# Reordering a head's softmax pipeline and its tail, with the output weights loaded in long rows, in a decode attention and MLP kernel

## The chip, the cores and the metric

The kernel runs on one core of one Trainium2 chip. The metric is the device time of one execution in microseconds (us). Executions of one kernel agree within about 0.4%.

## The reference, cut to what matters

```
x: 4 x 576;  32 query heads, 16 key/value heads, head size 128, last 2048 of 8192 positions
xn = layernorm(x)
q  = xn @ wq                                  # 576 x 4096
o  = softmax(q k^T / sqrt(128)) v             # per batch and head
A  = o.reshape(4, 4096) @ wo                  # 4096 x 576
B  = xn + gelu(layernorm(xn) @ w3) @ w4       # with one token the shifted branch is zero
out = x + A + B
```

Inputs and output are bf16. Little is computed with each byte. K and V alone are 67.1 MB, the weights about 20 MB.

## The kernel before: the parts that matter

K and V come in tiles of 2 MB, one per key/value head. Each of 128 partitions receives 16384 contiguous bytes. A head goes through three stages in three successive rounds of one loop. In round `t` K of head `t` is transposed on DVE and multiplied with q into a score bank. The softmax of head `t-1` runs, with its exponentials on ACT, and V of head `t-2` is multiplied on PE. The names in the profile: `kn` and `vn` are the tiles of K and V, `kt` is K transposed, `S` a score bank in PSUM (the memory that PE writes to), `mx`, `mxT` and `m` are steps of the maximum, `dg` is a diagonal of minus the maximum, which a matmul subtracts from `S`, `pt` are the exponentials, `O` the V products, `on` the normalised head output and `acc` the sum of the output. The mask matmul opens a score bank and writes a large negative number where query and key belong to different batches. DVE is VectorE, ACT is ScalarE, PE is TensorE and PEld its weight load.

```python
kvp = ctx.enter_context(tc.tile_pool(name="kv", bufs=NKV))                 # 7
ps_s = ctx.enter_context(tc.tile_pool(name="ps_s", bufs=2, space=PSUM))    # score banks
wo_src = A_wo.rearrange("(h d) n -> d h n", d=P)
def load_wo(p):              # 8 heads; a partition gets 8 separate rows of 1152 B
    t = wop.tile([P, WOH, D], BF16, tag="wo", name="wo_sb")
    nc.sync.dma_start(out=t[:], in_=wo_src[:, p * WOH:(p + 1) * WOH, :])
# ... cut ...
def pv(h, s):                # a quarter of the V products needs all four groups of exponentials
    for c in range(s * SC, (s + 1) * SC):
        nc.tensor.matmul(out=O_ps[h][:, 0:NJ], lhsT=vn[:, c, :], rhs=pt[:, c, :], ...)
# ... cut ...
for t in range(Hkv + LAG + 1):
    hm = t - 1; hv = t - LAG                    # LAG = 2
    for s in range(NSL):                        # four quarters
        if t < Hkv:
            k_transpose(t, s)                   # DVE, 3 kt buffers
            if s == 0: k_mask(t)                # PE, first write of head t's score bank
            k_scores(t, s)                      # PE
        if 0 <= hv - 1 < Hkv and s == 0: o_norm(hv - 1)
        if 0 <= hm < Hkv:
            if s == 0: sm_max(hm)               # DVE
            elif s == 1: sm_maxT(hm)            # PE mxT, DVE m and dg
            elif s == 2: sm_sub(hm); sm_exp(hm, 0); sm_exp(hm, 1)
            else: sm_exp(hm, 2); sm_exp(hm, 3)  # 16 exponentials in all, ACT
        if 0 <= hv < Hkv: pv(hv, s)
        if 0 <= hv - 1 < Hkv and s == 0: o_proj(hv - 1)
        # ... the MLP's first half runs in round 7 ...
for lo, hi in zip(W4_PIECES, W4_PIECES[1:]):
    mlp_out(lo, hi)                             # w4, in 5 pieces, after all heads
```

In the timelines below each engine runs its instructions in the order of these calls (PE runs L255, L275, L285 as the loop has them), so where a call stands in this loop decides what it may hold up.

## Time and profile before

| | before |
|---|---|
| time, median of 3 | 225.9 us |
| span of the profiled execution | 224.6 us |
| bytes read | 87.17 MB |
| last data packet of w4 lands (packet records of the trace) | 213.7 us |
| last w4 matmul ends | 221.4 us |
| mask matmul to mask matmul, heads 9 to 15 | 10.27 us |

The first lines are from the page: busy time of each engine with its share of the span.

```profile
span 224.6 us, 6358 instructions
...
PE 121.2 (54%) x2861; PEld 93.1 (41%) x2861; DVE 114.6 (51%) x214; ACT 70.3 (31%) x258; POOL 4.1 (2%) x13
```

No compute engine is busy for more than 54%. The view by windows gives, for each stretch of time, busy time by engine, the granted clock, the share of the 16 DMA engines' time and the rate. Here are stretches with a wo load (25 to 35 and 166 to 176 us), one with caches only, and the end.

```profile
core 0: us, PE busy (x) PEld busy (x) DVE busy (x) ACT busy (x) POOL busy (x), PEclk, DMA share, GB/s
25.00:35.00 10.00, 5.41 (x105) 3.58 (x105) 8.74 (x15) 1.28 (x1) 0.00 (x0) 1.00 1.03 399
36.00:56.00 20.00, 10.60 (x250) 7.75 (x250) 11.87 (x18) 8.59 (x32) 0.00 (x0) 1.00 1.00 424
166.00:176.00 10.00, 5.77 (x148) 4.45 (x147) 6.24 (x10) 4.30 (x16) 0.00 (x0) 1.00 1.04 404
208.00:214.00 6.00, 2.94 (x64) 2.07 (x61) 1.02 (x5) 4.30 (x16) 0.00 (x0) 1.00 0.53 219
214.00:224.60 10.60, 6.66 (x225) 5.97 (x222) 0.90 (x4) 0.00 (x0) 0.00 (x0) 0.98 0.01 4
```

The loads are saturated until 208 us, at 424 GB/s, or about 400 where wo's small packets are among them. Then come more than 10 us in which nearly nothing is loaded. The Trainium skill (page "Perfetto Trace Analysis", Engine Utilization, Roofline) puts the ceiling of a lone core at about 435 GB/s by its DMA engines. This trace, at 424 to 427, is near it.

Two rounds of the timeline show how a head's work hangs together. The columns are start and duration in us, engine, line and operation, and in brackets the idle time before it and who ended it.

```profile
171.25 4.47 ACT L292 ACTIVATE pt<-S 32x128 bf16<-32x128 f32 x16 [5.81 <-issue]
...
173.39 0.68 DVE L270 TENSOR_REDUCE mx<-S 128x8 f32<-128x512 f32 x1
...
175.77 0.58 PE L255 MATMUL S<-negbig,ohT 4*128 4x512 bf16 x1 [2.99 <-ACT pt L292]
...
178.14 0.37 PE L275 MATMUL mxT<-ident_f,mx 128*8 128x128 f32 x1
...
178.55 0.28 DVE L277 TENSOR_REDUCE m<-mxT 8x1 f32<-8x128 f32 x1 [3.33 <-PE mxT L275]
...
179.00 3.48 DVE L249 STREAM_TRANSPOSE kt<-kn 128x1024 int32<-128x1024 int32 x3
...
180.83 0.60 PE L285 MATMUL S<-dg,ones_bf 8*128 8x512 bf16 x1
...
181.51 4.47 ACT L292 ACTIVATE pt<-S 32x128 bf16<-32x128 f32 x16 [5.80 <-issue]
...
186.04 0.58 PE L255 MATMUL S<-negbig,ohT 4*128 4x512 bf16 x1 [3.00 <-ACT pt L292]
```

This is a ring. The exponentials end, and the mask matmul (L255), which waited 3.0 us for its bank, starts. Scores and mxT (L275) follow on PE, then m on DVE, which waited 3.3 us for it. Then come transposes, the subtraction (L285) and the next exponentials, 10.27 us later. Two cache tiles take 2 x 2.097 MB / 425 GB/s = 9.87 us, so this ring is slower than the loads. The chain of waits that ended last agrees: exponentials, the last V products, and all of w4 in one lump.

```profile
213.42 0.28 ACT pt L292
...
215.88 0.41 PE O L303 x16
...
217.17 4.28 PE acc L237 x148
...
221.47 0.31 DVE fin L421
```

### The profile page before, as it was taken

Reading aid. Unit: us, or ns where it says so; the run is one execution under the profiler, and the core shown is the slowest. Engines: PE = TensorE matmul, PEld = TensorE weight load, DVE = VectorE, ACT = ScalarE, POOL = GpSimd, SP = SyncE. Lnnn points to the kernel's source line nnn. Section 1 sums busy time; section 2 is a strip of 40 time slices with the busy share of each in tenths; the row PEclk is TensorE's granted clock in tenths of the full one; section 3 lists DMA queues with packets and bytes.
Section 4 is the critical chain, followed back from the end, with each engine's and each line's share of the span. In section 5 each row is a group of like instructions: output and inputs, shape, how many; then the busy total and the mean of one; then the engine's idle time right before and its main releaser. Section 6 shows DMA issues by size and latency. Waiting matters only on the chain. (4 is left out here: it accounts for less than half of the span.)

```text
span 224.6 us, 6358 instructions
## 1 busy us (share of the span) xinstructions
PE 121.2 (54%) x2861; PEld 93.1 (41%) x2861; DVE 114.6 (51%) x214; ACT 70.3 (31%) x258; POOL 4.1 (2%) x13
## 2 busy tenths in 40 slices
PE   0451454545474144475995547474755546475584
PEld 0440132333352033253994435353534334354373
DVE  5217898284840449073404875564738483742110
ACT  0000023451707006134070070716344261707700
POOL 5000000000000000000000000000000000000000
PEclk9999999999999999999999999999999999999999
DMA  6999999999999999999999999999999999999600
GB/s 215 425 435 426 429 384 417 432 423 432 429 414 428 423 413 399 420 426 429 426 420 423 390 418 420 435 426 432 417 419 389 423 423 429 416 421 415 248 4 4
DMA packets 10707, 87.58 MB, mean 390 GB/s; under 512 B 820, under 2 KB 4920, under 8 KB 5432
## 3 DMA queue, kind: packets, MB, share of 16 engines
q1 hardware_dynamic: 10664, 87.17, 93.5%
q8 instruction: 22, 0.36, 0.6%
q14 instruction: 5, 0.04, 0.0%
q10 hardware_dynamic: 16, 0.00, 0.0%
HBM read 87.17 MB, written 0.00 MB: 388 GB/s over the span
## 5 line engine op out<-in xcount | busy, mean ns | idle before, releaser
L292 ACT ACTIVATE pt<-S 32x128 bf16<-32x128 f32 x256 | 68.7, 269 | 106.9 <-issue 65.0
L249 DVE STREAM_TRANSPOSE kt<-kn 128x1024 int32<-128x1024 int32 x64 | 75.7, 1213 | 9.2 <-DMA kn<-in_A_k_cache_dram 9.2
L263 PEld LDWEIGHTS <-kt 128*128 128x128 bf16 x1024 | 33.1, 105 | 83.9 <-DVE kt L249 45.5
L263 PE MATMUL S<-qz,kt 128*128 128x32 bf16 x1024 | 39.0, 189 | 30.0 <-DVE kt L249 30.0
L303 PE MATMUL O<-pt,vn 128*128 128x8 bf16 x1024 | 38.2, 169 | 11.3 <-DMA vn<-in_A_v_cache_dram 5.7
L303 PEld LDWEIGHTS <-vn 128*128 128x128 bf16 x1024 | 34.8, 105 | 19.9 <-issue 13.1
L277 DVE TENSOR_REDUCE m<-mxT 8x1 f32<-8x128 f32 x16 | 4.4, 278 | 54.4 <-PE mxT L275 54.4
L255 PE MATMUL S<-negbig,ohT 4*128 4x512 bf16 x16 | 9.3, 583 | 39.8 <-ACT pt L292 39.8
L306 PE MATMUL O<-pt,ones_bf 128*128 128x64 bf16 x128 | 17.1, 226 | 0.0
L334 PE MATMUL AB<-ln2T,w_sb 128*128 128x4 bf16 x144 | 11.5, 201 | 0.0
L292 ACT ACT_TABLE_LOAD x1 | 1.3, 1283 | 32.5 <-DVE mx L270 32.5
L334 PEld LDWEIGHTS <-w_sb 128*128 128x128 bf16 x144 | 11.3, 161 | 0.2 <-issue 0.2
L315 DVE TENSOR_REDUCE dn<-O 128x8 f32<-128x64 f32 x16 | 3.5, 220 | 14.9 <-PE O L306 14.9
L270 DVE TENSOR_REDUCE mx<-S 128x8 f32<-128x512 f32 x16 | 10.8, 676 | 0.0
L285 PE MATMUL S<-dg,ones_bf 8*128 8x512 bf16 x16 | 9.6, 601 | 0.1
L306 PEld LDWEIGHTS <-ones_bf 128*128 128x128 bf16 x128 | 8.4, 104 | 0.0
L336 PE MATMUL AB<-ln2T,w_sb 128*128 128x4 bf16 x36 | 7.3, 202 | 0.0
L237 PE MATMUL acc<-wo_sb,on 128*4 128x144 bf16 x128 | 6.6, 302 | 0.8 <-DVE on L319 0.8
L275 PE MATMUL mxT<-ident_f,mx 128*8 128x128 f32 x16 | 6.0, 374 | 0.0
L336 PEld LDWEIGHTS <-w_sb 128*128 128x128 bf16 x36 | 5.8, 162 | 0.0
L186 PE MATMUL AB<-xnT,wq_sb 128*128 128x4 bf16 x128 | 4.0, 167 | 3.2 <-DMA wq_sb<-in_A_wq_dram 3.0
L186 PEld LDWEIGHTS <-wq_sb 128*128 128x128 bf16 x128 | 3.8, 104 | 3.4 <-DMA wq_sb<-in_A_wq_dram 3.1
(66 smaller groups left out, 49.9 us busy)
## 6 DMA issues: line engine op xcount, KB each, us to landing
kn<-in_A_k_cache_dram SPq DMA_DIRECT2D x16, 2048.0 KB, 19.9
vn<-in_A_v_cache_dram SPq DMA_DIRECT2D x16, 2048.0 KB, 26.8
wo_sb<-in_A_wo_dram SPq DMA_DIRECT2D x4, 1152.0 KB, 28.0
w_sb<-in_B_w_dram SPq DMA_DIRECT2D x2, 2304.0 KB, 32.9
wq_sb<-in_A_wq_dram SPq DMA_DIRECT2D x4, 1024.0 KB, 4.8
w_sb<-in_B_w_dram SPq DMA_DIRECT2D x3, 1296.0 KB, 26.6
w_sb<-in_B_w_dram SPq DMA_DIRECT2D x2, 576.0 KB, 32.2
w_sb<-in_B_w_dram SPq DMA_DIRECT2D x1, 720.0 KB
```

The costliest lines, as they stand in the source:

```text
L186: nc.tensor.matmul(out=q_ps[:, h, :], lhsT=wq_sb[:, j * NQ + h * Dh:j * NQ + (h + 1) * Dh], rhs=xnT[:, j, :], start=False, stop=False, ski ...
L237: nc.tensor.matmul(out=acc[i * QD:i * QD + B, :], lhsT=lhsT, rhs=rhs[:, i * CW:(i + 1) * CW], start=False, stop=False, skip_group_check=True)
L249: nc.vector.transpose(out=kt[:], in_=src)
L255: nc.tensor.matmul(out=S_ps[h][:].rearrange("p g k j -> p (g k) j"), lhsT=ohT[:], rhs=nb, start=True, stop=False, skip_group_check=True)
L263: nc.tensor.matmul(out=S_ps[h][:, s * (SC // NQD) + g].rearrange("p k j -> p (k j)"), lhsT=kt[:, ib, g * NQD:(g + 1) * NQD, e:2 * QD:2].re ...
L270: nc.vector.reduce_max(out=mx[:], in_=S_ps[h][:].rearrange("p g k j -> p j (g k)"), axis=AX.X)
L285: nc.tensor.matmul(out=S_ps[h][:].rearrange("p g k j -> p (g k) j"), lhsT=ones_bf[0:NJ, :], rhs=dg, start=False, stop=False, skip_group_ch ...
L292: nc.scalar.activation(out=PT[h][kb * QD:(kb + 1) * QD, :, c4, :], in_=S_ps[h][c4 * QD:(c4 + 1) * QD, :, kb, :], func=ACT.Exp, scale=scale)
L303: nc.tensor.matmul(out=O_ps[h][:, 0:NJ], lhsT=vn[:, c, :], rhs=pt[:, c, :], start=(c == 0), stop=False, skip_group_check=True)
L306: nc.tensor.matmul(out=O_ps[h][:, NJ:], lhsT=ones_bf[:], rhs=pt[:, c:c + DG, :].rearrange("p c j -> p (c j)"), start=False, stop=False, sk ...
L334: nc.tensor.matmul(out=g_ps[:, i, :], lhsT=w3[:, j * F + e * (F // 2) + f0:j * F + (e + 1) * (F // 2):NFH], rhs=ln2T[:, j, :], start=False ...
L336: nc.tensor.matmul(out=g_ps[:, i, :], lhsT=w3[:, KJ * F + f0:KJ * F + F // 2:NFH], rhs=ln2T[:, KJ + e, :], start=False, stop=False, skip_g ...
```

## The change

There are three intents. First, the loop is reordered so that a head no longer waits for the one before it: three score banks, the mask behind a quarter of V products, V products by exponential group, the subtraction a quarter earlier. Second, w4 is consumed as it lands, and head 15's projection slips in between. Third, wo is loaded in rows of 9216 B, which puts its rows on other partitions than the head outputs. Eight selection matmuls per four key/value heads copy the head outputs to all candidate places, and a mask with a reduce picks one. The diff, cut, and with the loop's guards left out:

```diff
-    ps_s = ctx.enter_context(tc.tile_pool(name="ps_s", bufs=2, space=PSUM))
+    ps_s = ctx.enter_context(tc.tile_pool(name="ps_s", bufs=3, space=PSUM))
-    wo_src = A_wo.rearrange("(h d) n -> d h n", d=P)
+    wo_src = A_wo.rearrange("(s p i) n -> s p (i n)", p=P, i=WOR)          # WOR = 8
-        nc.sync.dma_start(out=t[:], in_=wo_src[:, p * WOH:(p + 1) * WOH, :])
+        nc.sync.dma_start(out=t[:].rearrange("p i n -> p (i n)"), in_=wo_src[p])
+    sel_wo = const.tile([P, WOR, WOH, WOD], BF16)                          # 2 KB per partition
+    nc.gpsimd.tensor_copy(out=sel_wo[:], in_=ident_bf[:]....to_broadcast([P, WOR, WOH, WOD]))
+    own = const.tile([P, WOH], F32)
     # pv
-        for c in range(s * SC, (s + 1) * SC):
-            nc.tensor.matmul(..., lhsT=vn[:, c, :], rhs=pt[:, c, :], ...)
+        for g in range(CG):                  # quarter s needs exponential group s alone
+            nc.tensor.matmul(..., lhsT=vn[:, g * NQD + s, :], rhs=pt[:, g, s, :], ...)
+    def o_spread(h):   # 8 matmuls  R[:, i] = sel_wo[:, i]^T @ on   (once per 4 heads)
+    def o_pick(h):     # DVE: mk = R * own; op = sum over heads of mk
     # ... cut ...
-    for t in range(Hkv + LAG + 1):
+    for t in range(Hkv):
+        for s in range(NSL):
+            k_transpose(t, s)
+            if s == 0:   sm_max(hm); o_norm(hv - 1)
+            elif s == 2: o_pick(hv - 1)
+            pv(hv, s)
+            if s == 0: k_mask(t)
+            k_scores(t, s)
+            if s == 0:   sm_maxT(hm)
+            elif s == 1: sm_sub(hm); four sm_exp(hm, c4); o_spread(hv - 1)
+            elif s == 3: o_proj(hv - 1)
+    # tail: softmax of head 15 between V products of 14, then V of 15, then
+    mlp_out(*pieces[0]); o_spread(hl); o_pick(hl); mlp_out(*pieces[1]); o_proj(hl)
+    for lo, hi in pieces[2:]: mlp_out(lo, hi)
```

More of the change, by code (lines that the diff above doesn't have):

```diff
@@ L97 @@
     kv_tiles = {}
-    wo_src = A_wo.rearrange("(h d) n -> d h n", d=P)
     WOH = 8
+    WOR = WOH
+    WOD = P // WOH
+    WOQ = WOH // rep
+    wo_src = A_wo.rearrange("(s p i) n -> s p (i n)", p=P, i=WOR)
     def load_kv(kind, h):
@@ L108, in load_wo @@
     def load_wo(p):
-        t = wop.tile([P, WOH, D], BF16, tag="wo", name="wo_sb")
-        nc.sync.dma_start(out=t[:], in_=wo_src[:, p * WOH:(p + 1) * WOH, :])
+        t = wop.tile([P, WOR, D], BF16, tag="wo", name="wo_sb")
+        nc.sync.dma_start(out=t[:].rearrange("p i n -> p (i n)"), in_=wo_src[p])
         wo_tiles[p] = t
@@ L222 @@
                                 op0=ALU.add, op1=ALU.mult)
+    sel_wo = const.tile([P, WOR, WOH, WOD], BF16)
+    nc.gpsimd.tensor_copy(out=sel_wo[:], in_=ident_bf[:].rearrange("p (d i) -> p i d", i=WOR).unsqueeze(2)
+                          .to_broadcast([P, WOR, WOH, WOD]))
+    own = const.tile([P, WOH], F32)
+    nc.vector.reduce_sum(out=own[:], in_=ident_f[:].rearrange("p (h d) -> p h d", h=WOH), axis=AX.X)
     xsum = const.tile([B, D], F32)
@@ L300, in pv @@
         vn = kv_tiles["V", h]
-        pt = PT[h][:].rearrange("p g c j -> p (g c) j")
-        for c in range(s * SC, (s + 1) * SC):
-            nc.tensor.matmul(out=O_ps[h][:, 0:NJ], lhsT=vn[:, c, :], rhs=pt[:, c, :], start=(c == 0), stop=False,
-                             skip_group_check=True)
-        for c in range(s * SC, (s + 1) * SC, DG):
-            nc.tensor.matmul(out=O_ps[h][:, NJ:], lhsT=ones_bf[:],
-                             rhs=pt[:, c:c + DG, :].rearrange("p c j -> p (c j)"), start=False, stop=False,
-                             skip_group_check=True)
+        pt = PT[h][:]
+        for g in range(CG):
+            nc.tensor.matmul(out=O_ps[h][:, 0:NJ], lhsT=vn[:, g * NQD + s, :], rhs=pt[:, g, s, :],
+                             start=(g == 0 and s == 0), stop=False, skip_group_check=True)
+        for g in range(0, CG, DG):
+            nc.tensor.matmul(out=O_ps[h][:, NJ:].rearrange("p (c j) -> p c j", j=NJ), lhsT=ones_bf[:],
+                             rhs=pt[:, g:g + DG, s, :], start=False, stop=False, skip_group_check=True)
         if s == NSL - 1:
@@ L317, in o_norm @@
         nc.vector.reciprocal(out=rd[:], in_=dn[:])
-        on = small.tile([P, rep, B], BF16, tag="on")
-        nc.vector.tensor_tensor(out=on[:].rearrange("p r b -> p b r"), in0=o[:, 0:NJ].rearrange("p (b r) -> p b r", r=rep),
-                                in1=rd[:].rearrange("p (b r) -> p b r", r=rep), op=ALU.mult)
-        st["on", h] = on
-    def o_proj(h):
-        on = st.pop(("on", h))
-        for r in range(rep):
-            hq = h * rep + r
-            acc_matmuls(on[:, r, :], wo_tiles[hq // WOH][:, hq % WOH, :])
+        k = h % WOQ
+        if k == 0:
+            st["on"] = small.tile([P, WOH, B], BF16, tag="on", name="on")
+        nc.vector.tensor_tensor(out=st["on"][:, k * rep:(k + 1) * rep, :].rearrange("p r b -> p b r"),
+                                in0=o[:, 0:NJ].rearrange("p (b r) -> p b r", r=rep),
+                                in1=rd[:].rearrange("p (b r) -> p b r", r=rep), op=ALU.mult)
+    def o_spread(h):
+        if h % WOQ < WOQ - 1:
+            return
+        on = st.pop("on")
+        R = ps_m.tile([P, WOR, WOH, B], F32, tag="m", name="R")
+        for i in range(WOR):
+            nc.tensor.matmul(out=R[:, i].rearrange("p h b -> p (h b)"),
+                             lhsT=sel_wo[:, i].rearrange("p h d -> p (h d)"),
+                             rhs=on[:].rearrange("p h b -> p (h b)"), start=True, stop=True)
+        st["R"] = R
+    def o_pick(h):
+        if h % WOQ < WOQ - 1:
+            return
+        mk = small.tile([P, WOR, WOH, B], BF16, tag="mk")
+        nc.vector.tensor_tensor(out=mk[:], in0=st.pop("R")[:],
+                                in1=own[:].unsqueeze(1).unsqueeze(3).to_broadcast([P, WOR, WOH, B]), op=ALU.mult)
+        op = small.tile([P, WOR, B], BF16, tag="op")
+        with nc.allow_low_precision("one term is not zero"):
+            nc.vector.reduce_sum(out=op[:], in_=mk[:].rearrange("p i h b -> p i b h"), axis=AX.X)
+        st["op"] = op
+    def o_proj(h):
+        if h % WOQ < WOQ - 1:
+            return
+        op = st.pop("op")
+        for i in range(WOR):
+            acc_matmuls(op[:, i, :], wo_tiles[h // WOQ][:, i, :])
     def mlp_g(lo, hi):
@@ L367, in flush_loads @@
             kind, h = order[pos["n"]]
-            if kind == "V" and h % (WOH // rep) == 0:
-                load_wo(h // (WOH // rep))
+            if kind == "V" and h % WOQ == 0:
+                load_wo(h // WOQ)
             load_kv(kind, h)
@@ L380 @@
     G_AT = 7
-    for t in range(Hkv + LAG + 1):
+    for t in range(Hkv):
         hm = t - 1
-        hv = t - LAG
+        hv = t - 2
         for s in range(NSL):
-            if t < Hkv:
-                k_transpose(t, s)
-                if s == 0:
-                    k_mask(t)
-                k_scores(t, s)
-            if 0 <= hv - 1 < Hkv and s == 0:
-                o_norm(hv - 1)
-            if 0 <= hm < Hkv:
-                if s == 0:
-                    sm_max(hm)
-                elif s == 1:
+            k_transpose(t, s)
+            if s == 0:
+                if hm >= 0:
+                    sm_max(hm)
+                if hv - 1 >= 0:
+                    o_norm(hv - 1)
+            elif s == 2:
+                if hv - 1 >= 0:
+                    o_pick(hv - 1)
+            if hv >= 0:
+                pv(hv, s)
+            if s == 0:
+                k_mask(t)
+            k_scores(t, s)
+            if s == 0:
+                if hm >= 0:
                     sm_maxT(hm)
-                elif s == 2:
+            elif s == 1:
+                if hm >= 0:
                     sm_sub(hm)
-                    sm_exp(hm, 0)
-                    sm_exp(hm, 1)
-                else:
-                    sm_exp(hm, 2)
-                    sm_exp(hm, 3)
-            if 0 <= hv < Hkv:
-                pv(hv, s)
-            if 0 <= hv - 1 < Hkv and s == 0:
-                o_proj(hv - 1)
+                    for c4 in range(NQD):
+                        sm_exp(hm, c4)
+                if hv - 1 >= 0:
+                    o_spread(hv - 1)
+            elif s == 3:
+                if hv - 1 >= 0:
+                    o_proj(hv - 1)
             if t == G_AT:
@@ L411 @@
                     mlp_act()
-        if t < Hkv:
-            pos["free"] += 1
-        if 0 <= hv < Hkv:
+        pos["free"] += 1
+        if hv >= 0:
             pos["free"] += 1
         flush_loads()
-    for lo, hi in zip(W4_PIECES, W4_PIECES[1:]):
+    hl = Hkv - 1
+    sm_max(hl)
+    o_norm(hl - 2)
+    pv(hl - 1, 0)
+    sm_maxT(hl)
+    pv(hl - 1, 1)
+    sm_sub(hl)
+    for c4 in range(NQD):
+        sm_exp(hl, c4)
+    pv(hl - 1, 2)
+    pv(hl - 1, 3)
+    o_norm(hl - 1)
+    for s in range(NSL):
+        pv(hl, s)
+    o_norm(hl)
+    pieces = list(zip(W4_PIECES, W4_PIECES[1:]))
+    mlp_out(*pieces[0])
+    o_spread(hl)
+    o_pick(hl)
+    mlp_out(*pieces[1])
+    o_proj(hl)
+    for lo, hi in pieces[2:]:
         mlp_out(lo, hi)
```

## The prediction

> **What bounds it now.** The loads. The page gives 87.17 MB at 388 GB/s over a span of 224.6 us; the view by windows shows the 16 DMA engines at a share of 1.00 to 1.04 in every window from 25 to 208 us, at 424 to 427 GB/s where only caches stream. The last packet of w4 ends near 213.7 us (packet records), then about 11 us of tail follow.
>
> Compute is no bottleneck by its sums (DVE 51%, PE 54%, ACT 31%), but it is a chain. In the timeline each head takes 10.27 us: 16 exponentials 4.5 us, then the mask matmul waits for that score bank (idle 3.0 us, released by the last exponential), scores, mxT (DVE idle 3.3 us for it), m, dg, three transposes of 1.2 us, the subtraction, the next exponentials. Two caches at 425 GB/s take 9.87 us, so compute never catches up: K of head 15 has landed near 185 us, its transposes run at 194.5 to 201.9. The chain of waits ends with exponentials until 213.7, V products, the normalisation, then all 144 w4 matmuls in one lump of 4.05 us (217.36 to 221.4), fin 0.31, and 2.85 us of output and end.
>
> **What the change does.**
> 1. wo: 4096 packets of 1152 B (median 54 ns) become 512 of 9216 B. Interpolated from this trace's 8192 B (309 ns) and 10368 B (392 ns) packets, one takes about 350 ns: 14.2 us of 16-engine time become 11.2, 3.0 saved. By wall time, the four 10 us windows with wo run at 399 to 404 instead of 425 GB/s: 2.2 saved. I take 2.3. The Trainium skill ("DMA: Bandwidth & Descriptors", Why small descriptors are slow) names a fixed cost per packet and per descriptor; the two sizes above agree in direction. All of it is on the critical path.
> 2. Third score bank, mask after V products, V products by exponential group: the 3.0 us mask wait goes. Summing DVE (4 x 1.22 transposes, 0.68, 0.59, 0.50 and gaps), I estimate 7 to 8 us per head when data is there. Compute catches up and waits for DMA; the worth is the lag at the end.
> 3. Tail: head 15 should finish about 2 to 3 us after V of head 15 lands (near 199), before most of w4 is there. After w4's last piece, 16 matmuls (0.45 us) instead of 7.7 us from last packet to last matmul. About 7 us saved.
> 4. Added: per 4 heads, 8 selection matmuls of 32 columns (about 0.25 us), a mask multiply and a reduce of 128x256 (estimate 0.35 us each, from the 0.68 us reduce of 512); 32 wo matmuls of 28 ns pitch as before, in one lump. Off the critical path.
>
> **Sum.** Last packet 213.7 - 2.3 = 211.4; landing 0.2, matmuls 0.6, fin 0.35, end 2.85: span 215.4; plus 1.3 (225.9 timed against the span 224.6): **216.7 us**, range 215.2 to 219.3. Chances: faster by over 2% 0.94, within 2% 0.05, slower 0.01.
>
> **What would show it.** Packets of 9216 B near 350 ns, no dip below 415 GB/s in mid-kernel; transposes waiting for K's DMA, V products for V's DMA late in the run; head period equal to the DMA's 9.9 us; mask wait gone; last w4 matmuls waiting for DMA; chain ending in DMA rather than exponentials.
>
> **What would make it wrong.** Head period still above 9.9 us (transposes queued behind sm_max on DVE, or PE in its new order waiting for V before scores), leaving lag at the end; DMA engines ending more unevenly on w4; wo rows not streaming at the big packets' rate.

## More of the kernel before

The kernel before was run again beside every group of experiments. Its medians were 225.97, 226.59, 226.40 and 226.25 us, so differences below about half a microsecond against it carry little.

## The result, and the profile after

The kernel after takes 216.26 us (median of 4, 216.21 to 216.34) against 225.97 of before. The ratio is 0.9566, interval 0.9546 to 0.9586. Ratios here are the mean time of one kernel's runs over that of the other's of the same rounds, so they are not quite the ratio of the medians quoted.

| | before | after |
|---|---|---|
| time | 225.97 us | 216.26 us |
| last data packet | 213.7 us | 209.8 us |
| from there to the end of the last w4 matmul | 7.7 us | 1.1 us |
| from there to the end of the span | 3.2 us | 3.7 us |
| head 15's last K transpose begins | 200.7 us | 192.7 us |
| mean 16384 B packet | 618.7 ns | 613.3 ns |

The page and the windows after:

```profile
span 214.6 us, 6449 instructions
...
PE 121.0 (56%) x2893; PEld 94.9 (44%) x2893; DVE 118.0 (55%) x223; ACT 70.1 (33%) x258; POOL 6.1 (3%) x14
```

```profile
25.00:35.00 10.00, 5.18 (x98) 3.38 (x99) 9.19 (x15) 1.28 (x1) 0.00 (x0) 1.00 1.00 425
36.00:56.00 20.00, 12.53 (x310) 9.66 (x309) 14.77 (x23) 11.54 (x44) 0.00 (x0) 1.00 1.01 431
166.00:176.00 10.00, 4.37 (x120) 3.57 (x117) 6.22 (x10) 4.28 (x16) 0.00 (x0) 1.00 1.02 435
194.00:208.00 14.00, 10.88 (x324) 8.76 (x321) 3.63 (x14) 7.50 (x28) 0.00 (x0) 1.00 0.92 385
208.00:214.60 6.60, 1.42 (x36) 0.89 (x35) 0.31 (x1) 0.00 (x0) 0.00 (x0) 0.56 0.10 37
```

The dips of the wo windows are gone (425 and 435 where it was 399 and 404). The window with caches alone also rose, from 424 to 431, and the mean 16384 B packet of K and V fell from 618.7 to 613.3 ns. Nothing in the plan of the change touches these. This becomes the main question below. The rate now falls only at the end of the loads, and the stretch after it is short. (PEclk is the clock that was granted to PE. It fell to 0.56 in that last stretch, but only 36 matmuls lie in it. Of the four executions the two with a mean clock of 1.000 took 216.21 and 216.26 us, those with 0.986 and 0.989 took 216.34 and 216.26.)

The timeline in mid-kernel:

```profile
154.78 0.50 PEld L313 LDWEIGHTS <-vn 128*128 128x128 bf16 x16 [2.92 <-DMA vn<-in_A_v_cache_dram]
154.78 0.59 PE L313 MATMUL O<-pt,vn 128*128 128x8 bf16 x16 [2.81 <-DMA vn<-in_A_v_cache_dram]
...
155.43 0.60 PE L265 MATMUL S<-negbig,ohT 4*128 4x512 bf16 x1
...
159.78 4.49 ACT L302 ACTIVATE pt<-S 32x128 bf16<-32x128 f32 x16 [5.26 <-issue]
...
164.66 0.59 PE L313 MATMUL O<-pt,vn 128*128 128x8 bf16 x16 [2.93 <-DMA vn<-in_A_v_cache_dram]
...
165.31 0.60 PE L265 MATMUL S<-negbig,ohT 4*128 4x512 bf16 x1
```

Both rounds start with PE waiting 2.8 to 2.9 us for V's DMA; over the whole run V products wait for it 12 times, 41.7 us in all. The mask (L265) waits for nothing. These two rounds are 9.88 us apart and the two before them 9.76 and 9.77, the pace of the loads. The tail and the chain that ended last:

```profile
207.14 0.73 PE L247 MATMUL acc<-w_sb,gT 128*4 128x144 bf16 x36 [1.17 <-DMA w_sb<-in_B_w_dram]
...
208.88 0.77 PE L247 MATMUL acc<-w_sb,gT 128*4 128x144 bf16 x20 [1.00 <-DMA w_sb<-in_B_w_dram]
...
210.26 0.65 PE L247 MATMUL acc<-w_sb,gT 128*4 128x144 bf16 x16 [0.61 <-DMA w_sb<-in_B_w_dram]
...
210.96 0.31 DVE L480 CAST fin<-acc 128x144 bf16<-128x144 f32 x1 [5.87 <-PE acc L247]
```

```profile
152.04 30.72 DMA kn<-in_A_k_cache_dram
...
182.78 27.43 DMA w_sb<-in_B_w_dram
...
210.26 0.68 PE acc L247 x16
```

Three pieces of w4 each wait for their DMA. The chain is now loads back to mid-kernel (152.04 on, one load of K and one of w4, each counted from issue to landing). Where before it was exponentials, PE now only adds 0.7 us after the last load has landed.

### The profile page after: what moved, and what is told of

It is laid out like the page before. It is cut to its first block, busy times and chain, and to the rows that moved or that the text cites. A ratio compares the mean times of both kernels' runs of the same rounds, so it can differ in the third digit from the quotient of the medians.

```text
span 214.6 us, 6449 instructions
## 1 busy us (share of the span) xinstructions
PE 121.0 (56%) x2893; PEld 94.9 (44%) x2893; DVE 118.0 (55%) x223; ACT 70.1 (33%) x258; POOL 6.1 (3%) x14
## 5 line engine op out<-in xcount | busy, mean ns | idle before, releaser
L259 DVE STREAM_TRANSPOSE kt<-kn 128x1024 int32<-128x1024 int32 x64 | 74.3, 1205 | 11.4 <-DMA kn<-in_A_k_cache_dram 11.4
L313 PE MATMUL O<-pt,vn 128*128 128x8 bf16 x1024 | 37.4, 169 | 43.2 <-DMA vn<-in_A_v_cache_dram 41.7
L273 PEld LDWEIGHTS <-kt 128*128 128x128 bf16 x1024 | 33.6, 106 | 36.1 <-DVE kt L259 30.4
L265 PE MATMUL S<-negbig,ohT 4*128 4x512 bf16 x16 | 9.6, 601 | 0.0
L247 PE MATMUL acc<-w_sb,gT 128*4 128x144 bf16 x144 | 4.8, 294 | 2.8 <-DMA w_sb<-in_B_w_dram 2.8
L247 PEld LDWEIGHTS <-gT 128*4 128x4 bf16 x144 | 3.4, 104 | 3.6 <-issue 3.5
```

The source lines that it names most:

```text
L247: nc.tensor.matmul(out=acc[i * QD:i * QD + B, :], lhsT=lhsT, rhs=rhs[:, i * CW:(i + 1) * CW], start=False, stop=False, skip_group_check=True)
L259: nc.vector.transpose(out=kt[:], in_=src)
L265: nc.tensor.matmul(out=S_ps[h][:].rearrange("p g k j -> p (g k) j"), lhsT=ohT[:], rhs=nb, start=True, stop=False, skip_group_check=True)
L273: nc.tensor.matmul(out=S_ps[h][:, s * (SC // NQD) + g].rearrange("p k j -> p (k j)"), lhsT=kt[:, ib, g * NQD:(g + 1) * NQD, e:2 * QD:2].re ...
L313: nc.tensor.matmul(out=O_ps[h][:, 0:NJ], lhsT=vn[:, g * NQD + s, :], rhs=pt[:, g, s, :], start=(g == 0 and s == 0), stop=False, skip_group ...
```

## The experiments

Twelve kernels were run, each timed in three rounds beside the kernel before. Names say which part of the change is in them. "Offset" is where the destination of K, V, w and wo tiles starts in each partition, past a multiple of 256 B. It is read from the compiled programs. The groups ran on three chips; the ratio to the kernel before, run on the same chip, takes out what differs between them.

| kernel | loop and tail | wo packets | offset | time, us | last packet, us | mean 16 KB packet, ns |
|---|---|---|---|---|---|---|
| before | old | 1152 B | 32 | 225.97 to 226.59 | 213.7 | 618.7 |
| wo_rows_only | old | 9216 B | 32 | 224.96 | 212.1 | 618.1 |
| banks3_only | old, 3 banks | 1152 B | 32 | 221.84 | 213.9 | 618.8 |
| tail_only | old loop, new tail | 1152 B | 32 | 225.22 | 213.9 | 618.7 |
| sched_only | new | 1152 B | 32 | 220.62 | 214.0 | 618.7 |
| after_no_spread | new | 9216 B | 32 | 218.41 | 211.9 | 618.1 |
| after_shift32 | new | 9216 B | 32 | 218.43 | 212.0 | 618.0 |
| after_shift128 | new | 9216 B | 128 | 217.64 | 211.2 | 616.8 |
| sched_aligned | new | 1152 B | 0 | 217.42 | 210.8 | 613.5 |
| after_wo2304 | new | 2304 B | 0 | 216.67 | 210.4 | 613.3 |
| after_again | new | 9216 B | 0 | 216.18 | 209.7 | 613.5 |
| after_2banks | new, 2 banks | 9216 B | 0 | 216.34 | 209.8 | 613.4 |
| after_oldtail | new loop, old tail | 9216 B | 0 | 216.05 | 209.8 | 613.5 |

Three of them (wo_rows_only, after_no_spread, after_wo2304) apply head outputs to the wrong rows of wo on purpose. The comparison with the reference passed all the same, so it is too coarse to vouch for this term. That holds for the kernel after as well.

### 1. The wo rows alone, in the old order

```diff
-    wo_src = A_wo.rearrange("(h d) n -> d h n", d=P)
+    wo_src = A_wo.rearrange("(s p i) n -> s p (i n)", p=P, i=WOH)
-        nc.sync.dma_start(out=t[:], in_=wo_src[:, p * WOH:(p + 1) * WOH, :])
+        nc.sync.dma_start(out=t[:].rearrange("p i n -> p (i n)"), in_=wo_src[p])
```

> The kernel before with nothing changed but the address pattern of the wo load (9216 B rows; head outputs still applied as if wo lay as before, so the result is wrong on purpose). Theory: in the kernel before the head chain of 10.27 us per head sets the time, not the loads; the last w4 packet lands 2 to 4 us earlier (about 210 to 211.7 us), the head period stays 10.27 and the time stays 225.9 within 0.5 us. Rival: the loads set the time already, so that all of the bytes' gain is seen: 222.1 to 223.7 us.

Measured: 224.96 us, ratio 0.9938 (0.992 to 0.9955), last packet at 212.1. Neither number fits exactly. The theory holds from head 8 on: the period stays 10.27 to 10.28 us in heads 9 to 15 of both kernels. The gain arises earlier. The masks of heads 7 and 15 (counted from 0) both come 1.0 us earlier (102.6 instead of 103.6 us, 195.3 instead of 196.3). In the kernel before, K of head 5 arrives late behind the large w3 load, and there the chain does wait for the loads:

```profile
76.26 1.25 DVE L249 STREAM_TRANSPOSE kt<-kn 128x1024 int32<-128x1024 int32 x1 [8.73 <-DMA kn<-in_A_k_cache_dram]
```

Here the same transposition starts at 75.7 us, and head 7's at 98.2 instead of 99.2. The other half microsecond is in the w4 lump, whose 144 matmuls took 3.56 us here and 4.05 before. In both traces they first start 30.0 ns apart and later 15.6 ns apart. The step comes after about 116 matmuls in the kernel before and after about 80 here, and 36 x 14.4 ns = 0.52 us is the difference. What sets the moment of the step stays open. So the old order is bound by loads up to about head 7 and by its own ring afterwards. Of wo's four loads only the early ones counted.

### 2. The new order alone, wo as before

This is the kernel after with `load_wo` and the projection per head of the kernel before, and no selection.

> The kernel after with the old wo load (1152 B packets) and the old projection per head. Theory: once the schedule is fixed the loads set the time, so undoing the wo rows costs what they save in loading. If that is my 2.3 us: 218.6 us. If all of the 3.8 us by which the last packet came earlier is wo's: 220.1 us, last packet near 213.7. Rival 1: wo's rows are worth nothing, 216.3. Rival 2: the wo rows with their selection matmuls are the main gain and the schedule little: 223 or more.

Measured: 220.62 us, ratio 0.9743 (0.9727 to 0.9759), last packet at 214.0. The number is nearest to "all is wo's", but the later runs show that this reading is wrong: half of the step from here to the kernel after is not wo's. What this run does show is the order's own share. With the last packet unmoved (213.7 and 214.0), the last w4 matmul ends 1.1 us after it instead of 7.7:

```profile
213.06 0.77 PE L239 MATMUL acc<-w_sb,gT 128*4 128x144 bf16 x20 [0.53 <-DMA w_sb<-in_B_w_dram]
...
214.47 0.65 PE L239 MATMUL acc<-w_sb,gT 128*4 128x144 bf16 x16 [0.65 <-DMA w_sb<-in_B_w_dram]
```

By time this is 5.8 us (0.0257 of 226.4): 6.6 from the stretch after the last packet, less some 0.8 because the last packet (by 0.3) and the end of the span (by 0.45) came a little later.

### 3. The third bank alone, in the old order

```diff
-    ps_s = ctx.enter_context(tc.tile_pool(name="ps_s", bufs=2, space=PSUM))
+    ps_s = ctx.enter_context(tc.tile_pool(name="ps_s", bufs=3, space=PSUM))
```

> The kernel before with three score banks instead of two, nothing else. Theory: the mask matmul's 3.0 us wait for the exponentials goes, but the V products right behind it still need all four exponential groups of the same head, so about 2 us of the wait moves to them; head period about 9.9 to 10.2, time 222.5 to 225.5 us. Rival: the missing bank is all there is to the 10.27 us; the period falls to the loads' 9.87, the lag at the end goes, and the time falls to about 222, only the w4 lump left at the end.

Measured: 221.84 us, ratio 0.979 (0.9767 to 0.9812; whether the gain is over 2% is unclear). The wait did move to the V products as I thought, but it shrank on the way, so the period fell to 9.25 us, less than the loads' 9.87. The expected time was wrong and the rival's right. The view of waits (total us, times, longest) has the moved wait:

```profile
PE O L303 <- ACT pt L292: 19.4, 22, 1.0
```

In the kernel before, the same view has

```profile
PE S L255 <- ACT pt L292: 39.8, 13, 4.0
...
PE O L303 <- ACT pt L292: 5.6, 6, 1.0
```

The first of these, the mask's wait for the exponentials, is gone here. With the ring faster than the loads, the chain catches up after the MLP's round, and in round 14 V products wait for V's DMA:

```profile
181.97 0.59 PE L303 MATMUL O<-pt,vn 128*128 128x8 bf16 x16 [3.53 <-DMA vn<-in_A_v_cache_dram]
```

### 4. The new tail alone

> The loop of before over 16 heads, then the tail of after (with the projection per head). Theory: head 15's exponentials still end near 213.7 us because the loop's lag stays, its V products follow until 216.3, and only the 0.8 us wait of the projection in front of w4 is hidden: 225.1 us (224.6 to 225.6). Rival: the order of the tail is worth the 7 us by itself: 218.5 to 220.

Measured: 225.22 us, ratio 0.994 (0.992 to 0.996). The time is the theory's, but that was set against 225.9; against the kernel before of the same rounds it saves 1.4 us, 0.6 more than the theory had. The loop's lag stays: the w4 matmuls begin at 215.6 us, after the last packet (213.9), so the tail's order cannot use the early w4 pieces.

### 5. The kernel after again

> The kernel after once more, on the chip of these four runs. Its K and V packets took 613.3 ns on the mean in its first profile, against 618 to 619 in every other kernel so far (1.4 us of loading), so part of the 4.4 us between it and sched_only may be the chip's and not wo's. Theory: it is the chip's; here the mean is 617 to 619, the last packet lands at 210.8 to 211.4 and the time is 217.2 to 217.8. Rival: it is the kernel's; 612 to 614 ns again, 209.8 and 216.3 us.

Measured: 216.18 us, 613.5 ns, last packet at 209.7. The theory fell: the faster packets belong to the kernel, not to the chip of that day.

### 6. Without the selection, mask and reduce

This is sched_only with the wo load of experiment 1.

> The kernel after without selection matmuls, mask and reduce: projection per head from rows that no longer fit (wrong on purpose). Theory: the added work is off the critical path; the same as after_again within 0.4 us. Rival: the added PE and DVE work and the lumped projection cost about 1.9 us per four heads; 1 us or more faster than after_again.

Measured: 218.41 us, ratio 0.9649 (0.9633 to 0.9664), which is 2.2 us slower than after_again though it does less work. Both expectations missed. All packets are slow again (618.1 ns), so the work that was removed had something to do with the loads. The compiled programs give a candidate. The selection's tiles stand in front of the load buffers, and without them the first K tile starts at byte 34848 of each partition (136 x 256 + 32), as in the kernel before. With them it starts at 38144 (149 x 256). The Trainium skill (page "DMA: Bandwidth & Descriptors", How a descriptor splits into AXI transactions) says that the first transaction of a descriptor that does not start on a multiple of 256 B begins at the boundary below, and that the bytes before the start are fetched unused and still cost beats (steps of 32 B on the bus). The page tells it of reads. Here K and V are read from the same places in all kernels and only the destination moved.

### 7. Wo in packets of 2304 B

```diff
-    wo_src = A_wo.rearrange("(s p i) n -> s p (i n)", p=P, i=WOR)
+    wo_src = A_wo.rearrange("(s g p e) n -> s p g (e n)", p=P, e=2, g=WOR // 2)
```

> The kernel after with wo loaded in 2048 packets of 2304 B instead of 512 of 9216 B (rows land elsewhere, wrong on purpose). A straight line through 54 ns at 1152 B and 348 ns at 9216 B gives 12 ns fixed and 96 ns at 2304 B: 12.3 us of loading instead of 11.1. Theory (a fixed cost per packet): last packet and time 1.2 us later than in after_again, up to 1.7 if the wall gain is more than the packets' sum as between sched_only and after. Rival (only packets under 2 KB are slow): same as after_again within 0.4 us.

Measured: 216.67 us, 0.5 more than after_again; the last packet 0.6 later. The mean packet took 93.2 ns. With 347.0 ns at 9216 B this gives a slope of 0.0367 ns per byte and 8.6 ns fixed. The 1152 B packets of sched_aligned (51.1 ns) lie on this line (42.3 + 8.6 = 50.9). At that slope 16 engines would move 436 GB/s, an estimate from these two sizes. My line had put the fixed part at 12 because its 54 ns came from the kernel before, whose destinations are at offset 32. So there is a fixed cost, but it is smaller than I had it, and at 2304 B it is worth only 0.5 us here.

### 8. The new loop with the old tail

The loop runs on to round 18 with guards, and `mlp_out` of all pieces follows it.

> The new loop run on for three more rounds as the old loop was, and w4 only after all heads: the new tail's order undone. Theory: by the time the last w4 packet lands the heads have long been done (205.7 us in the first profile against 209.8), so the order of the tail is worth nothing once the loop keeps up: same as after_again within 0.4 us. Rival: the tail's order is worth 1.4 us as it was in tail_only.

Measured: 216.05 us. The tail's order is worth nothing once the loop keeps up.

### 9 and 10. The kernel after, moved by 32 and by 128 bytes

```diff
+    const.tile([P, 16], BF16, name="pad")     # 32 B, unused; [P, 64] for 128 B
     x_bf = const.tile([B, D], BF16)
```

> The kernel after with one unused 32 B tile in front, so that every load's destination starts 32 B past a multiple of 256 as in the kernel before, instead of on one. Theory: after_no_spread was 2.2 us slower than after_again because without the 2 KB selection tile its K, V, wo and w tiles fell back to that offset, not because of any work: K and V packets 618 ns instead of 613.4, wo 352.5 instead of 347, last packet 211.9, time 218.4 us. Rival: the place of the tiles is nothing, the selection work itself or its timing speeds the loads up: 216.2 us, 613.4 ns.

> The same with a 128 B tile: destinations 128 B past a multiple of 256. Theory (the boundary that counts is 256 B[...] whatever the offset): as after_shift32, 618 ns and 218.4 us. Rival (a boundary of 64 or 128 B): as after_again, 613.4 ns and 216.2 us.

Measured: 218.43 us with 32 B (ratio 0.9647, 0.9631 to 0.9663; 618.0 ns, last packet 212.0), and 217.64 us with 128 B (0.9615, 0.96 to 0.9629; 616.8 ns, 211.2). An unused tile of 32 B costs 2.25 us, 1.0%. Work, order and bytes are the same in these and in after_again. The last piece of w4 lands that much later. First after_shift32, then after_again:

```profile
212.49 0.65 PE L248 MATMUL acc<-w_sb,gT 128*4 128x144 bf16 x16 [0.87 <-DMA w_sb<-in_B_w_dram]
```

```profile
210.18 0.65 PE L247 MATMUL acc<-w_sb,gT 128*4 128x144 bf16 x16 [0.78 <-DMA w_sb<-in_B_w_dram]
```

The chip is no rival: after_2banks, at offset 0 and on the same chip as after_shift32, took 216.34 us. The pad moves the tiles that the engines compute with as well, but K's second tile shows that this is not needed for the effect. It loads from 18.7 us on, before the first transposition of K at 26.1, and all its 128 packets took 611 ns in after_again, while 614 and 621 ns are the commonest times in after_shift32. The theory of the place holds for these loads. It is no rule for every packet: the 512 packets of 8192 B of wq, loaded first into a tile at the same offset, have a median of 309 ns at offsets 0, 32 and 128 alike. Why they are spared stays open. The 128 B run is between the two expectations: offset 128 does cost, but about two thirds of what offset 32 costs. "Whatever the offset" was wrong.

### 11. The same from the other side

```diff
+    const.tile([P, 112], BF16, name="pad")    # 224 B, unused, in sched_only
```

> sched_only (new schedule, wo still in 1152 B packets, no selection) with an unused 224 B tile that brings its destinations to a multiple of 256 B. Theory: K and V packets 613.4 ns instead of 618.7, last packet about 2 us earlier than 214.0, time 218.2 to 218.7 us against 220.6. Rival: 220.6.

Measured: 217.42 us, ratio 0.9606 (0.9592 to 0.962), 613.5 ns. It is 3.2 us faster than sched_only, more than expected: the 1152 B packets gain too (55.2 to 51.1 ns), and there are 4096 of them.

### 12. The kernel after with two banks

> The kernel after with two score banks instead of three. Theory: in the new order the exponentials start a quarter of a head earlier and the mask stands behind V products, so the mask seldom waits; the loads still set the time: 216.2 to 217.0 us. Rival: the third bank is what lets the loop keep up, as banks3_only gave half of the whole gain in the old order: 218 us or more.

Measured: 216.34 us, no different from after_again. The mask does wait for exponentials again (8.8 us in 6 waits, below), and while the chain catches up its rounds (heads 10 to 13) take 8.85 to 8.95 us. In after_again one of 7.5 us is enough, and the others are at the loads' pace. Both are faster than the loads, so it doesn't matter:

```profile
PE S L265 <- ACT pt L302: 8.8, 6, 2.0
```

## Why the prediction was right or wrong

The time (216.7 predicted, 216.26 measured) and the direction were right, and so was the mechanism of a loop that keeps up with the loads. That the sum came so near is partly luck, because its errors cancelled. The last packet came 1.6 us before the 211.4 predicted. Against that, from there to the last matmul it took 1.1 us instead of 0.8, from `fin` to the end 3.3 instead of 2.85, and time and span differ by about 1.75 us instead of 1.3. The 1.3 set a median of 225.9 us against the span of one execution that itself took 226.53.

- **What bounded the kernel before.** "The loads", and then "compute never catches up". The first half of this is right only up to about head 7. From head 8 on the ring of 10.27 us sets the time, and wo_rows_only shows it: the last packet came 1.6 us earlier and only about 1.4 us of time came of it, of which 1.0 us was gained by head 7 and the rest in a faster w4 lump. After the reordering the loads bind throughout.
- **wo.** "I take 2.3" is the term that failed, in that it was meant to be all of the loads' gain. The last packet came 3.9 us earlier. The wo rows by themselves were sized right: at the old offset they give 220.62 to 218.43, 2.2 us. At offset 0 they give 217.42 to 216.18, 1.2 us. The rest, 218.43 to 216.18 = 2.25 us, came from where the tiles stand: the load destinations fell on multiples of 256 B, because the selection tiles moved them. The diff says nothing of this, and I had not looked at addresses.
- **Third bank, mask after V products.** "the 3.0 us mask wait goes" is right, and so is the pace after it, "Compute catches up and waits for DMA" (rounds of 9.76 to 9.88 us, two of them with PE waiting 2.8 and 2.9 us for V). That the third bank has a part in it is not so in the new order (after_2banks), though in the old order it alone brings 4.7 us. Which of the other reorderings carries the loop (V products by group, the mask's place, the earlier subtraction) was not separated and stays open.
- **Tail.** "About 7 us saved" was 6.6 to the last matmul, and 5.8 by time (sched_only). The credit given to the tail's order was wrong. It is the loop that no longer lags: the old tail under the new loop costs nothing, and the new tail under the old loop saves 1.4 us. The end of the span takes 3.7 us after the last matmul instead of 3.2, which I had not foreseen. It lies after the last packet of the output: from there to the end it is 1.8 us in all ten kernels with the new loop, the one with the old tail and the ones without selection included, and 1.35 in the four with the old loop. What in the new loop adds it stays open.
- **Added work.** "Off the critical path" is right: after_shift32 with it and after_no_spread without it take 218.43 and 218.41 us at the same offset.

The sum by runs, from about 226.4: order 5.8, wo rows 2.2, place of the tiles 2.25, which leaves 216.2.

## What to carry to other kernels

Before crediting a shorter load, find out for each stretch whether loads or a ring of dependent steps sets the pace, by comparing the period of a round with the time that its bytes take. Here the change of data layout paid in full (2.2 us against 1.4) only after the ring had been made faster than the loads. When a kernel is bound by loads, look at the start addresses of the destination tiles modulo 256. A few added or removed constants can move every later tile, and here this was worth as much as all of wo's longer rows.

## What the Trainium skill lacked or had wrong

- Page "DMA: Bandwidth & Descriptors", How a descriptor splits into AXI transactions: it speaks of the bytes that are read. Here a shift of the destinations in SBUF by 32 B, with the same sources, cost 618.0 ns instead of 613.5 per 16384 B packet and 353.5 instead of 347.0 per 9216 B packet, 1.0% of the time. By the page's counting, applied to the destination, offset 128 should waste more beats than offset 32 (516 against 513 for 16384 B, an estimate by its rule). The runs show the opposite order, 616.8 ns against 618.0. The wq packets of 8192 B showed no cost at all (309 ns at offsets 0, 32 and 128). The 4096 K and V packets alone account for 4096 x 4.5 ns / 16 = 1.15 of the 2.25 us, all load packets together for 1.7 (after_shift32 against after_again); the rest is in no load packet's time.
- The same page, Why small descriptors are slow, names a fixed cost per packet (in cycles, for a small one) and per descriptor but no time by size in this range. Packets of 1152, 2304 and 9216 B (51.1, 93.2 and 347.0 ns) lie on a line with 8.6 ns fixed. Going from 1152 to 9216 B for 4.7 MB of 87 was worth 1.2 us of 217.
- Page "Runtime: NRT & Kernel Launch", Instruction fetch mechanics, calls the cost of crossing a block of instructions mostly hidden. It does not speak of the loads beside it. The traces have 22 instruction packets of 16 KB in the loads' time. They took 1071 ns each at offset 32 (after_shift32) and 929 ns at offset 0 (after_again), so 20 to 24 us of one engine's time in all. Whether they cost the kernel any time was not tested.
- No page that I used names the allocation of tiles in SBUF as something that a change of unrelated constants can spoil. An unused tile of 32 B cost 2.25 us.
